# Unread transposes in TensorE's planned idle time, in the first ten head pairs of an attention and gated-FFN kernel

## The chip, the cores and the metric

The kernel runs on one core of a Trainium2 chip, as one program with one launch. The metric is the device time of an execution in microseconds; the figure shown is the median of several executions. The profile comes from one execution of its own, whose time and span are given below. In its views PE is TensorE (PEld its weight loads), DVE is VectorE, ACT is ScalarE, POOL is GpSimd, and SP issues most DMAs.

## What is computed

Attention over 8 batches of 8 heads, 576 positions and 64 channels a head, with rotary embedding of q and k, and after it a gated layer on the 512 joined channels, all in float32:

```python
q_rot, k_rot = (rotate(q), rotate(k))
scores = scale * np.matmul(q_rot, k_rot.transpose(0, 1, 3, 2))
scores = scores - np.max(scores, axis=-1, keepdims=True)
attn = np.exp(scores)
attn = attn / (np.sum(attn, axis=-1, keepdims=True) + 1e-09)
x = np.matmul(attn, v)                    # heads joined: (B, S, 512)
...
for k in range(K):                        # K = 5 taps, causal, one weight a channel
    gate_pre += conv_w[k][None, None, :] * xp[:, k:k + S, :]
gate = 1.0 / (1.0 + np.exp(-gate_pre))
val = x @ w_val
return gate * val @ w_out
```

## The kernel before

The work goes by **pairs** of heads: 32 pairs, four to a batch. A pair passes through these steps:

- **Rope.** k and q of the pair are loaded (L238), multiplied by tables and added (L255, L259, mostly on GpSimd), and split into a rounded high part (ScalarE, L262) and the rest (L266, GpSimd). The first pair's k is done on VectorE in part.
- **Scores.** `s_mm` (L283), five jobs a pair: four with rows of 128 for both heads (12 matmuls each), one with the last 64 rows of both heads (6 matmuls). A score tile takes two PSUM banks, and there are two of them. For each of nine tiles VectorE takes the negated maximum (L289), and ScalarE the exponential with its sum (L302).
- **Transposes.** `t_mm` calls `transpose` (L308): up to four 128x128 transposes of the exponentials into one PSUM bank of the pool `psT`, which a copy on ScalarE (L349) or VectorE (L351) takes to SBUF. This pool has four banks with one tag, shared with the products with V, the transpose of the sums and the gated layer.
- **Product with V.** `pv_mm` (L363), four jobs, 40 matmul instructions a pair. The sums are inverted (L374, L375), transposed (`r_mm`, L379), written to DRAM and read back spread over the partitions; VectorE multiplies them in (`x_norm`, L402).
- **Gate.** Split of x (L410, L414), five taps (L424 and L427, VectorE for four), tanh (L432).

After each fourth pair the gated layer of the batch follows, two stages of eight output tiles, each in three parts of four matmuls (`f_mm`, L450), between the attention jobs of the next pairs. The weights come as 64-bit words and are decoded on VectorE, GpSimd and ScalarE (`decode`, L486 to L500) during the first pairs.

**The order is a planner's.** Every step is a job with an engine, a duration written by hand, a due time (the table `DUE`), and the data that it reads and writes. `Plan.order` goes through them like a small scheduler: it starts the earliest job that can start, with lags between engines and the counts of buffers, and it keeps each job's planned `start` and `end` in nanoseconds. `Plan.run` then calls the jobs' functions in that order, and each engine executes its instructions in the order in which they were called:

```python
    def run(self):
        for i in self.order():
            self.jobs[i][3](*self.jobs[i][4])
```

The planned times themselves go no further: on the chip the engines wait for each other's semaphores alone. In the plan the first TensorE job, a score job, starts at 14.35 us. `ident` is a 128x128 identity that GpSimd builds at the start.

Of the kernel before, what the change touches and what calls it, by code (L numbers as in the profile page):

```python
# [10 lines left out]
F32 = mybir.dt.float32  # L11
# [43 lines left out]
class Plan:  # L55
# [10 lines left out]
    LAG = {"PE": 200, "V": 130, "A": 135, "G": 90, "SP": 100}  # L66
    WAIT = {"PE": 100, "V": 100, "A": 100, "G": 130, "SP": 40}
    SWITCH = 145

    def __init__(self):  # L70
        self.jobs = []
# [34 lines left out]
    def order(self, due=None):  # L106
# [34 lines left out]
        while len(done) < n:  # L141
# [11 lines left out]
            if m and m != mode:  # L153
                ns += self.SWITCH
                mode = m
# [17 lines left out]
        self.start, self.end = start, end  # L173
        return done

    def run(self):
        for i in self.order():
            self.jobs[i][3](*self.jobs[i][4])


# [1 line left out]
def attn_gated_ffn(ctx: ExitStack, tc: tile.TileContext, q2, k2, v2, tab, w_val, conv_w, w_out, out, collect=None):  # L182
# [14 lines left out]
    V, A, G, T, SP = nc.vector, nc.scalar, nc.gpsimd, nc.tensor, nc.sync  # L197
# [10 lines left out]
    psT = ctx.enter_context(tc.tile_pool(name="psT", bufs=B["ps_t"], space=PSUM))  # L208

    ident = const.tile([128, 128], F32, name="ident")  # L210
# [13 lines left out]
    state = {}  # L224
# [66 lines left out]
    def s_exp(p, i):  # L291
# [7 lines left out]
        else:  # L299
# [2 lines left out]
        A.activation(out=pd.rearrange("p (b x) -> p b x", b=2), in_=st[f"s{i}"], func=AF.Exp, bias=st[f"nm{i}"], scale=1.0,  # L302
                     accum_out=sums[p % 2][:, col:col + 1])

    def transpose(p, key, srcs):
        bank = psT.tile([128, 512], F32, name="ps_t", tag="ps_t")
        for j, (src, rows) in enumerate(srcs):
            T.transpose(out=bank[0:rows, j * 128:(j + 1) * 128], in_=src, identity=ident)  # L308
        state[p]["b" + key] = bank

    def t_mm(p, key):


        st = state[p]
        if key == "m":
            transpose(p, key, [(st["pm"][:, j * 128:(j + 1) * 128], 128) for j in range(4)])
        elif key == "hm":
            transpose(p, key, [(st["pm"][:, 448:S], 128)])
        elif key[0] == "h":
            g = int(key[1])  # L320
            transpose(p, key, [(st[f"p{2 * g + n}"].rearrange("p h s -> p (h s)")[:, 512:640], 128) for n in range(2)])
        else:
            c, h = int(key) // 2, int(key) % 2
            transpose(p, key, [(st[f"p{c}"][:, h, h * D + j * 128:h * D + (j + 1) * 128], 128) for j in range(4)])
# [218 lines left out]
    plan = Plan()  # L543
# [32 lines left out]
    for p in range(NP):  # L576
        t = 9 * p
        par = p % 2
        xt = toks(f"x{par}#@", R2)
        for n in ("k", "q"):  # L580
            cut = 320 if n == "k" else G0
            for a, b in [(0, W)] if p else [(0, cut), (cut, W)]:
                x = b - a
# [33 lines left out]
        for key, w in [(str(i), i) for i in range(8)] + [("m", 8), ("h0", 3), ("h1", 7), ("hm", 8)]:  # L617
# [7 lines left out]
            b = f"ps_t/{p}{key}"  # L625
# [7 lines left out]
        for g in R2 if last else (None,):  # L633
            k = "l" + str(g) if last else ""
# [5 lines left out]
        for g in R2:  # L640
            n = G1 if g else G0
# [14 lines left out]
        else:  # L656
            for g, (a, b) in enumerate(((0, G0), (G0, S))):
                x = b - a
# [11 lines left out]
        b = p // PPB  # L670
        last = b == NB - 1
        for stage in range(2):
            for j in range(8):
# [5 lines left out]
                key = f"f{stage}" + "l" * last + str(j)  # L679
# [9 lines left out]
                x = hi - lo  # L689
# [9 lines left out]
    if collect is not None:  # L699
        return plan  # L700
    with tc.manual_schedule():
        plan.run()


# [36 lines left out]
def _program(arrays, batches):  # L741
    import concourse.bacc as _bacc

    nc = _bacc.Bacc("TRN2", target_bir_lowering=False, num_devices=1)
    args = [
        nc.dram_tensor(f"in_{n}", a.shape, mybir.dt.from_np(a.dtype), kind="ExternalInput").ap()
        for n, a in arrays.items()
    ]
    args.append(nc.dram_tensor("out_t", (batches, DM, S), F32, kind="ExternalOutput").ap())
    with tile.TileContext(nc, schedule_with_timeline_sim=True) as tc:  # L750
        attn_gated_ffn(tc, *args)
    return nc
# [9 lines left out]
```

## Time and profile before

| what | value |
|---|---|
| median of 3 runs | 790.36 us (790.29, 790.36, 795.87) |
| profiled execution, its own time | 788.1 us |
| its span, first to last instruction | 786.3 us |
| instructions | 16022 |
| TensorE busy | 723.4 us (92% of the span), 5889 matmuls |
| VectorE, ScalarE, GpSimd busy | 542.2, 507.6, 538.1 us (69%, 65%, 68%) |
| mean granted TensorE clock | 0.967 |

How to read the views. A row of the slices gives the busy share of each of 40 equal slices in tenths; the clock row gives the granted TensorE clock in the same way. A row of the waits names the engine and tile that waited, what ended the wait, the total, the number of waits and the longest. A row of the stretches gives start and end in us, length, then for each engine its busy time and the number of instructions, the granted clock, the DMA share and GB/s. A row of the timeline gives start and duration in us, engine, line, operation, output and inputs, shapes and count of a group of like instructions, and in brackets the idle time before it and what ended it. The chain of waits follows the work that ended last back from the end; by line it gives shares of the stretch that is asked for.

### The profile page before, as it was taken

What the parts mean: (1) busy time and instruction counts of PE and PEld (TensorE: products, weight loads), DVE (VectorE), ACT (ScalarE), POOL (GpSimd) and SP (SyncE); (2) the same over time, 40 slices, a digit from 0 to 9 for tenths busy, and PEclk for the clock granted to TensorE, in tenths of its full rate; (3) what the DMA queues carried; (4) which work ended last, traced back from release to release, by engine and by line L of the source; (5) the groups of instructions that cost most, each with busy time, mean ns of one, the idle gap of its engine ahead of it and who ended that gap; (6) DMA issues with size and microseconds to landing.
All of it is one profiled execution on the core that took longest, in us unless ns stands there. A gap on an engine that the chain in (4) does not pass through costs nothing.

```text
span 786.3 us, 16022 instructions
## 1 busy us (share of the span) xinstructions
PE 723.4 (92%) x5889; PEld 582.9 (74%) x5889; DVE 542.2 (69%) x871; ACT 507.6 (65%) x1182; POOL 538.1 (68%) x395
## 2 busy tenths in 40 slices
PE   0687677999999999999999999999999999999998
PEld 0454454776789877787779878787778877887788
DVE  4769695788957767657767777656766876756750
ACT  1564544667677767766687667766687668766642
POOL 3788686787888776787757766777757866872021
PEclk9897677999999999999999999999999999999999
DMA  8454142243444233433443332333442343320101
GB/s 217 95 138 105 41 105 75 62 110 88 109 117 117 78 101 85 107 93 93 123 115 88 79 114 86 77 94 103 121 109 85 79 123 86 94 70 31 46 33 62
DMA packets 92881, 73.76 MB, mean 94 GB/s; under 512 B 60633, under 2 KB 71426, under 8 KB 92802
## 3 DMA queue, kind: packets, MB, share of 16 engines
q1 hardware_dynamic: 91250, 71.51, 34.1%
q10 hardware_dynamic: 1552, 1.21, 0.6%
q8 instruction: 47, 0.77, 0.4%
q14 instruction: 32, 0.26, 0.1%
HBM read 63.10 MB, written 9.59 MB: 92 GB/s over the span
## 4 chain that ended last, share of the span: by engine, by line
PE 76%; DVE 9%; ACT 6%; DMA 3%; issue 2%; SPq 2%; POOL 1%; DVEq 0%; ACTq 0%; POOLq 0%
PE ps_f L450 24%; PE ps_t L308 18%; PE ps_s L283 17%; PE ps_a L363 17%; ACT p L302 4%; DVE nm L289 3%; DMA rb<-rd 2%; DVE g L427 2%; SPq L238 1%; ACT pt L349 1%; POOL k L266 1%; DMA qin<-in_q 1%; DVE sums L374 1%; DMA v<-in_v 1%; DVE x L402 0%
## 5 line engine op out<-in xcount | busy, mean ns | idle before, releaser
L289 DVE TENSOR_REDUCE nm<-ps_s 128x1 f32<-128x576 f32 x288 | 208.1, 751 | 109.0 <-PE ps_s L283 107.7
L302 ACT ACTIVATE p<-ps_s,nm 128x576 f32<-128x576 f32 x288 | 212.1, 740 | 82.9 <-DVE nm L289 76.4
L308 PE MATMUL ps_t<-ident,p 128*128 128x128 f32 x1312 | 203.4, 289 | 35.2 <-ACT p L302 34.0
L308 PEld LDWEIGHTS ps_t<-ident,p 128*128 128x128 f32 x1312 | 152.7, 146 | 74.1 <-ACT p L302 50.4
L283 PE MATMUL ps_s<-k,q 64*128 64x288 f32 (+1 forms) x1728 | 178.9, 319 | 22.3 <-ACT k L262 17.6
L349 ACT COPY pt<-ps_t 128x512 f32<-128x512 f32 (+2 forms) x288 | 135.6, 477 | 67.7 <-PE ps_t L308 65.2
L283 PEld LDWEIGHTS ps_s<-k,q 64*128 64x128 f32 (+1 forms) x1728 | 139.4, 193 | 53.8 <-issue 25.0
L363 PE MATMUL ps_a<-pt,v 128*64 128x320 f32 (+1 forms) x1280 | 172.5, 418 | 0.0
L427 DVE SCALAR_TENSOR_TENSOR g<-x,cw,g 128x576 f32<-128x576 f32 (+2 forms) x132 | 137.7, 1044 | 1.3 <-ACT g L424 0.6
L363 PEld LDWEIGHTS ps_a<-pt,v 128*64 128x64 f32 x1280 | 88.2, 140 | 63.6 <-issue 13.0
L255 POOL TENSOR_TENSOR qin<-qin,tab_q 128x640 f32<-128x640 f32 (+2 forms) x66 | 106.8, 1632 | 37.0 <-DMA qin<-in_q 34.4
L450 PE MATMUL ps_f<-y,wout_hi 128*128 128x288 f32 (+2 forms) x512 | 107.9, 302 | 0.0
L255 POOL TENSOR_TENSOR kin<-kin,tab_k 128x640 f32<-128x640 f32 (+1 forms) x63 | 99.7, 1593 | 9.9 <-DMA kin<-in_k 9.9
L351 DVE COPY pt<-ps_t 128x512 f32<-128x512 f32 (+1 forms) x128 | 77.2, 615 | 20.8 <-PE ps_t L308 20.0
L414 POOL TENSOR_TENSOR xl<-x,xh 128x576 fp32r<-128x576 f32 (+2 forms) x33 | 46.1, 1397 | 62.8 <-ACT xh L410 62.7
L465 POOL TENSOR_TENSOR y<-y,y 128x288 fp32r<-128x288 f32 (+2 forms) x64 | 52.3, 820 | 51.5 <-ACT y L462 51.5
L450 PEld LDWEIGHTS ps_f<-y,wout_hi 128*128 128x128 f32 x512 | 81.5, 188 | 1.5 <-issue 1.5
L450 PE MATMUL ps_f<-xh,wval_hi 128*128 128x288 f32 (+2 forms) x256 | 78.3, 307 | 0.0
L450 PE MATMUL ps_f<-y,wout_lo 128*128 128x288 f32 (+2 forms) x256 | 77.2, 302 | 0.0
L450 PE MATMUL ps_f<-xh,wval_lo 128*128 128x288 f32 (+2 forms) x256 | 76.5, 300 | 0.0
L450 PE MATMUL ps_f<-xl,wval_hi 128*128 128x288 f32 (+2 forms) x256 | 75.5, 296 | 0.0
L266 POOL TENSOR_TENSOR q<-qin,q 128x640 fp32r<-128x640 f32 (+2 forms) x33 | 50.3, 1524 | 27.3 <-ACT q L262 27.3
(65 smaller groups left out, 782.8 us busy)
## 6 DMA issues: line engine op xcount, KB each, us to landing
kin<-in_k SPq DMA_DIRECT2D x62, 288.0 KB, 4.3
qin<-in_q SPq DMA_DIRECT2D x31, 512.0 KB, 5.0
out_t<-o SPq DMA_DIRECT2D x56, 144.0 KB, 2.2
rb<-rd SPq DMA_DIRECT2D x31, 144.0 KB
v<-in_v SPq DMA_DIRECT2D x32, 128.0 KB, 4.0
v<-in_v SPq DMA_DIRECT2D x64, 64.0 KB, 2.3
rb<-rd SPq DMA_DIRECT2D x31, 128.0 KB, 2.9
qin<-in_q SPq DMA_DIRECT2D x64, 32.0 KB, 3.8
```

The lines of the kernel that those rows point to most:

```text
L255: eng.tensor_tensor(out=t[:, i, a:b], in0=t[:, i, a:b], in1=tabs[n][:, i, a:b], op=ALU.mult)
L266: eng.tensor_tensor(out=t[:, 1], in0=ins[n][:, 0, a:b], in1=t[:, 0].bitcast(F32), op=ALU.subtract)
L283: T.matmul(out=tiles[h][:, half, 0:288], lhsT=st["q"][rows, x, c * 128:c * 128 + 128], rhs=st["k"][rows, y, k0:k0 + 288], start=(i == 0), ...
L289: V.tensor_reduce(out=st[f"nm{i}"], in_=st[f"s{i}"], axis=AX.XY, op=ALU.max, negate=True)
L302: A.activation(out=pd.rearrange("p (b x) -> p b x", b=2), in_=st[f"s{i}"], func=AF.Exp, bias=st[f"nm{i}"], scale=1.0, accum_out=sums[p % 2 ...
L308: T.transpose(out=bank[0:rows, j * 128:(j + 1) * 128], in_=src, identity=ident)
L349: A.copy(out=dst, in_=src)
L351: V.tensor_copy(out=dst, in_=src)
L363: T.matmul(out=acc[HEAD[h], 0:n], lhsT=st["v"][:, j, h, :], rhs=st[f"pt{g}"][:, at_:at_ + n], start=(j == 0), stop=(j == 4))
L427: V.scalar_tensor_tensor(out=g, in0=x_sb[:, a + k:b + k], scalar=w, in1=g, op0=ALU.mult, op1=ALU.add)
L450: T.matmul(out=acc[:, 0:n], lhsT=wt[w][:, kc, ds], rhs=mv, start=(kc == 0 and i == 0), stop=(kc == NCH - 1 and i == 2))
L465: G.tensor_tensor(out=ffn[b][1][:, dc, lo:hi], in0=ffn[b, "y", dc, lo], in1=ffn[b][0][:, dc, lo:hi].bitcast(F32), op=ALU.subtract)
```

## The change

`run` gets two more arguments, the function `t_mm` and a new function `fill`. It goes through the planned order as before. Ahead of each TensorE job it takes the planned idle time since the end of the TensorE job before it (since 3000 ns for the first), subtracts 300 ns and divides by 110 ns; the first job gets 25 more. If that number is over 2, the last TensorE job ended before 230000 ns in the plan, and one of the next four TensorE jobs (this one included) is a `t_mm`, it calls `fill` with that number and with the pair and key of that `t_mm`. `fill` takes the PSUM bank that this `t_mm` would take later, and issues that many 128x128 transposes of the identity into the first 128 columns of it. `transpose` then uses the bank that is there, and overwrites it. Nothing reads what `fill` wrote.

```diff
     SWITCH = 145
+    FILL = (3000, 230000, 300, 110, 25)
...
-    def run(self):
-        for i in self.order():
+    def run(self, turn, fill):
+
+
+        order = self.order()
+        pe = [i for i in order if self.jobs[i][1] == "PE"]
+        t, k = self.FILL[0], 0
+        for i in order:
+            if self.jobs[i][1] == "PE":
+                n = int((self.start[i] - t - self.FILL[2]) / self.FILL[3]) + (0 if k else self.FILL[4])
+                turns = [x for x in pe[k:k + 4] if self.jobs[x][3] == turn]
+                if n > 2 and t < self.FILL[1] and turns:
+                    fill(n, *self.jobs[turns[0]][4])
+                t = self.end[i]
+                k += 1
             self.jobs[i][3](*self.jobs[i][4])
...
+    def fill(n, p, key):
+        st = state.setdefault(p, {})
+        if "b" + key not in st:
+            st["b" + key] = psT.tile([128, 512], F32, name="ps_t", tag="ps_t")
+        for _ in range(n):
+            T.transpose(out=st["b" + key][:, 0:128], in_=ident, identity=ident)
+
     def transpose(p, key, srcs):
-        bank = psT.tile([128, 512], F32, name="ps_t", tag="ps_t")
+        bank = state[p].get("b" + key)
+        if bank is None:
+            bank = psT.tile([128, 512], F32, name="ps_t", tag="ps_t")
...
     with tc.manual_schedule():
-        plan.run()
+        plan.run(t_mm, fill)
```

## The prediction

> **What bounds the kernel now.** I read the slices first, then TensorE's waits before and after 141 us, the granted clock in stretches of 3.41 us, single groups of matmuls at both clocks, and the chain of waits in each stretch at half clock.
>
> ```profile
> PE   0687677999999999999999999999999999999998
> PEclk9897677999999999999999999999999999999999
> ```
>
> Each slice is 19.7 us. In the first seven TensorE is neither full nor at full clock; then it is full to the end. Before 141 us it waits for these:
>
> ```profile
> PE ps_t L308 <- ACT p L302: 28.2, 15, 3.5
> PE ps_s L283 <- ACT k L262: 17.6, 1, 17.6
> PE ps_s L283 <- ACT p L302: 2.8, 4, 1.1
> PE ps_s L283 <- POOL k L266: 1.2, 1, 1.2
> ```
>
> and after it for almost nothing (its largest wait from 141.20 on, then its busy time in the same stretch):
>
> ```profile
> PE ps_t L308 <- ACT p L302: 5.8, 9, 1.4
> ...
> 141.20:786.30 645.10, 633.65 (x5316) 518.92 (x5314) 444.59 (x708) 440.93 (x1033) 435.73 (x315) 1.00 0.33 90
> ```
>
> So from 141 us on 633.65 of 645.10 us is TensorE's own work at clock 1.00, in a fixed order. What is won before 141 us arrives at the end; nothing can be won after it.
>
> **Do transposes keep the clock up?** Columns: stretch, its length, TensorE busy (matmuls), clock, DMA. All matmuls first, then only those that write transpose banks.
>
> ```profile
> 25.14:28.56 3.42, 2.01 (x17) 1.00 0.83 239
> 31.97:35.38 3.41, 1.64 (x14) 1.00 0.01 2
> 38.80:42.21 3.41, 3.39 (x16) 0.50 0.17 16
> ...
> 134.37:137.78 3.41, 1.63 (x19) 1.00 0.71 174
> ...
> 141.20:144.61 3.41, 2.00 (x17) 1.00 0.00 0
> ```
>
> ```profile
> 38.80:42.21 3.41, 2.10 (x9) 0.50 0.17 16
> ...
> 134.37:137.78 3.41, 0.03 (x1) 1.00 0.71 174
> ...
> 141.20:144.61 3.41, 1.36 (x11) 1.00 0.00 0
> ```
>
> The stretches with 1.64 and 1.63 us busy (48%) were followed by half clock, those with 2.01 and 2.00 (59%) were not. The one from 134.37 holds 1.60 us of other matmuls and hardly a transpose, and the clock fell; the one from 141.20 holds 1.36 us of transposes and 0.64 us beyond them, and it stayed. If transposes did not count, it would be the other way round. Likewise 38.80 to 42.21, at half clock and mostly transposes, brought the clock back. I take it that transposes count, that the clock falls below a share between 48 and 59%, and that a full stretch restores it.
>
> [...]
>
> **What one transpose costs at each clock.**
>
> ```profile
> 17.63 2.27 PE L283 MATMUL ps_s<-k,q 64*128 64x288 f32 x12 [17.63 <-ACT k L262]
> ...
> 33.67 1.38 PE L308 MATMUL ps_t<-ident,p 128*128 128x128 f32 x8 [1.86 <-ACT p L302]
> ...
> 40.85 0.45 PE L379 MATMUL ps_r<-ident,sums 128*128 128x128 f32 x1
> ...
> 44.00 1.07 PE L283 MATMUL ps_s<-k,q 64*128 64x288 f32 x12
> ...
> 51.90 1.25 PE L308 MATMUL ps_t<-ident,p 128*128 128x128 f32 x10
> ...
> 61.89 2.40 PE L308 MATMUL ps_t<-ident,p 128*128 128x128 f32 x10 [1.71 <-ACT p L302]
> ...
> 157.44 0.30 PE L379 MATMUL ps_r<-ident,sums 128*128 128x128 f32 x1 [0.56 <-DVE sums L375]
> ```
>
> One alone lasts 0.30 us at full and 0.45 at half clock, so the step from one to the next is (1.25 - 0.30)/9 = 0.106 us at full and (2.40 - 0.45)/9 = 0.217 at half. The first score job's 2.27 us, part of it a wait for k, against the later 1.07 points to half clock there too, though the clock row shows 9: its records seem to begin later. Ten transposes lose 48% of their time when the clock is full; a score job that waits for nothing loses (1.81 - 1.07)/1.81 = 41% (the rows of 138.79 and 134.90 below). I use 42%, as score jobs hold most of the chain.
>
> **What the change adds.** No instruction goes. The plan's order is as before; `run` counts the plan's idle time before each TensorE job. Worked through with the file's costs, its rule gives 30 groups, 499 transposes: 125 ahead of the first score job, 374 in 29 groups up to pair 8, most of 13 to 20 ahead of transposes that wait for the exponentials. Such a group is hidden where the trace waits: 16 fills ahead of the job at 33.67 take 16 x 0.106 = 1.7 us of 1.86 idle. Four planned gaps, three before the product with V and one before the small transpose of pair 2's sums, have no transpose among the next four jobs and stay empty. Where other jobs stand between fill and real transposes, they are score jobs, which use other banks; the fill may wait for its bank's copy, with that score job queued behind it. I cost this at 0 to 0.5 us a place and take 0, since the real gaps there end later than the copies.
>
> **The gain, by the chain of waits.** The stretches at half clock, by lines of the chain (share of each stretch): 17.60 to 25.14, 35.38 to 42.21, 59.28 to 66.10; 76.34 to 83.17; 113.89 to 117.30, 120.72 to 130.96, 137.78 to 141.20.
>
> ```profile
> by line: PE ps_s L283 44.1%; PE ps_t L308 25.6%; ACT p L302 11.2%; DVE nm L289 10.2%; DVE k L266 8.9%; issue 2.1%
> by line: issue 36.6%; POOL q L266 22.5%; PE ps_s L283 16.5%; DVE nm L289 11.3%; ACT q L262 9.1%; ACT p L302 3.2%; ACTq L262 0.6%; POOLq L491 0.2%; DVEq L289 0.2%
> by line: ACT p L302 22.9%; DVE sums L374 22.4%; PE ps_a L363 20.2%; PE ps_s L283 15.4%; DVE nm L289 11.1%; PE ps_r L379 6.6%; DVE sums L375 3.3%; issue 3.0%
> by line: DVE nm L289 30.9%; PE ps_s L283 21.3%; DVE g L427 17.7%; PE ps_t L308 16.4%; ACT p L302 12.4%; DVE pt L351 8.8%; issue 2.1%; DVEq L289 0.3%
> ...
> by line: PE ps_s L283 69.4%; PE ps_t L308 37.5%
> by line: PE ps_t L308 34.2%; PE ps_a L363 21.6%; PE ps_s L283 17.4%; ACT p L302 16.4%; DVE nm L289 14.1%; issue 2.2%; PE ps_r L379 2.1%; ACTq L302 0.2%; DVEq L289 0.1%
> by line: PE ps_s L283 50.8%; PE ps_t L308 50.7%
> ```
>
> TensorE on the chain: 5.3 + 1.1 + 2.9 = 9.3 us up to 72; 2.6 in pair 2; 3.4 + 7.7 + 3.4 = 14.5 after 104. At 42% these are 3.9, 1.1 and 6.1, in all 11.1: the upper end. What is late next decides how much arrives:
>
> ```profile
> 72.07 0.93 PE L283 MATMUL ps_s<-k,q 64*128 64x288 f32 x10 [1.21 <-POOL k L266]
> ...
> 96.58 6.85 PE L363 MATMUL ps_a<-pt,v 128*64 128x256 f32 x40
> 103.36 1.06 PE L283 MATMUL ps_s<-k,q 64*128 64x288 f32 x12
> ...
> 134.90 1.07 PE L283 MATMUL ps_s<-k,q 64*128 64x288 f32 x12
> ...
> 138.79 1.81 PE L283 MATMUL ps_s<-k,q 64*128 64x288 f32 x12
> ```
>
> ```profile
> 43.00:60.00 17.00, 13.63 (x115) 9.64 (x111) 9.36 (x16) 10.01 (x23) 15.76 (x12) 0.98 0.62 160
> ...
> 104.00:120.72 16.72, 9.84 (x61) 7.69 (x57) 15.76 (x20) 9.29 (x20) 15.19 (x11) 0.80 0.30 70
> ...
> 120.72:130.96 10.24, 8.49 (x41) 6.34 (x43) 5.90 (x11) 6.01 (x14) 5.32 (x5) 0.50 0.19 60
> ```
>
> - **To 72 us, 0 to 3.9, taken 1.4.** Even with the slow clock TensorE waited 1.21 us for GpSimd's k there, and GpSimd was busy 15.76 of 17.00 us. It profits only as far as its own inputs, behind ScalarE's exponentials, come earlier.
> - **Pair 2, 0 to 1.1, taken 0.6**, for the same reason.
> - **From 104 on, 4.7 to 6.1, taken 5.4.** VectorE is busy 15.76 of 16.72 us until 120.72, so half of the 1.4 us of the stretch from 113.89 is given back to it; from 120.72 on no other engine stands near (VectorE 5.90, ScalarE 6.01, GpSimd 5.32 of 10.24 us).
>
> Sum 7.4. Costs against it:
>
> ```profile
> 1.01 0.29 POOL masks.py:199 TENSOR_SCALAR_AFFINE_SELECT ident<-ident 128x128 f32<-128x128 f32 x1
> ```
>
> The first block can start when the identity is there, at 1.3 us. With one slow stretch (3.4 us, 16 fills) it ends at 1.3 + 3.4 + 109 x 0.106 = 16.3; with two (31 fills) at 1.3 + 6.8 + 94 x 0.106 = 18.1, against the first score job's 17.63: 0 to 0.5 late, taken 0.3. The 25 fills ahead of the job at 103.36, which did not wait, take 2.7 us; a full clock in the product with V before it (40 matmuls in 6.85 us, of which 3.66 at half clock, up to 100.24) frees 42% of 3.66, 1.5: 0 to 1.2, taken 0.5. Twelve fills in three small groups of pairs 4, 5 and 8 stand where TensorE is full: 0 to 1.3, taken 0.6. Sum 1.4.
>
> Net 7.4 - 1.4 = 6.0: the profiled execution's 788.1 (span 786.3 and 1.8 around it) becomes 782.1. The median shown is 790.36, 2.3 higher. Part of that may be the phase of the slow stretches, which would vanish; I carry 0.9 over: **783.0 us**.
>
> **Rivals.**
> - **Given back (0.22): 787 to 790.** GpSimd and VectorE, both over 90% busy in the rows above, set the pace to 120 us; then only the last stretches' gain remains, and the fills' upper costs (0.5 + 1.2 + 1.3 = 3.0) eat most of it. For it: the wait for POOL k. Against: the chain after 120.72 is three quarters TensorE.
> - **The clock still falls (0.15): 785 to 788.** The change doesn't do what it says where gaps stay empty or VectorE is later than planned. One empty gap as long as the waits of 1.71 and 1.86 us above brings a stretch to the 48 to 59% at which it falls. Half of the stretches left gives half of 7.4, less 1.4: a gain of 2.3.
> - **All of it (0.12): 777 to 780.** GpSimd's and VectorE's inputs come earlier by as much, and the 11.1 arrive less small costs.
> - **Slower (0.06): 801 or more.** [...]
>
> **How the numbers follow.** The forecast has 0.45, with its own range 780 to 787. One per cent, about what a measurement of this kernel can tell from no change, is 7.9 us, so "faster" begins at 782.5: just under half of the forecast (0.22) and all of "all of it" (0.12), and a little from the tails, 0.36. "Slower" is the last rival and a rest for a bank that I mis-judged, 0.07; within 1% is 0.57. The range, 778 to 791, leaves out the slower rival and half of "all of it".
>
> **What would show it.** TensorE has 5889 + 499 = 6388 matmuls; the clock row is 9 in every slice after the first one or two; ten transposes of pair 1 take 1.25 us, not 2.40; the job that began at 134.90 begins some 6 us earlier, and the rest keeps that lead. If the clock is full and the lead at 72 us is nil, GpSimd sets the pace there. The forecast is wrong if the first score job starts well after 18 us, if half-clock stretches remain beside the empty gaps, or if TensorE's waits before 141 us turn into waits of score jobs for k.

## The result, and the profile after

Over 13 executions of each, the median went from 792.6 to 787.75 us. The ratio is **0.9936, with a 95% interval of 0.9912 to 0.9961**: 4.9 us less, under one per cent. Measured again later (below, with the gaps that stayed empty) the ratio was 0.9916, 0.9887 to 0.9944, with 5.1 us between the medians. The median of before, 790.36 when the prediction was made, is 792.6 with ten more executions; single ones lie between 789.86 and 796.33. The profiled execution after took 785.75 us, against 788.1.

The page after: span and instructions, busy time, the slices of TensorE, VectorE and the clock.

```profile
span 783.9 us, 17018 instructions
...
PE 760.3 (97%) x6388; PEld 623.9 (80%) x6388; DVE 553.6 (71%) x871; ACT 507.8 (65%) x1182; POOL 539.3 (69%) x395
...
PE   8899898899999999999999999999999999999998
...
DVE  4869797878866777656767767656766876756750
...
PEclk9999999999999999999999999999999999999999
```

There are 6388 matmuls, as counted. The clock is full in all 40 slices where before it fell in five of the first seven, and TensorE is nearly full from the first slice on. But **VectorE**, with the same 871 instructions, is 11.4 us busier than before (542.2), and the span is only 2.4 us shorter. Both hold for this pair of executions only. Each kernel was profiled a second time, on one chip (the runs stand at the end of the experiments); there VectorE is busy 547.3 us in both, and the span is 5.9 us shorter. I call the two profiles shown so far the first pair, and those the second. TensorE's waits before 141.20 us, after:

```profile
PE ps_t L330 <- ACT p L315: 6.7, 5, 1.6
PE ps_r L401 <- DVE sums L397: 2.0, 1, 2.0
PE ps_t L323 <- POOL ident masks.py:199: 1.4, 1, 1.4
PE ps_s L296 <- ACT p L315: 1.0, 1, 1.0
PE ps_s L296 <- ACT k L275: 0.9, 1, 0.9
PE ps_s L296 <- POOL k L279: 0.7, 1, 0.7
```

The 28.2 us of waits for the exponentials are 6.7 now. That is not a gain in itself: the fills stand there instead.

**Transposes count for the granted clock.** The first two stretches of the block (start, length, TensorE busy with its matmuls, clock; only these transposes run until 17.9 us), and the block:

```profile
1.36:4.77 3.41, 3.41 (x16) 1.00 0.70 167
4.77:8.18 3.41, 3.41 (x32) 1.00 1.10 259
```
```profile
1.36 15.62 PE L323 MATMUL ps_t<-ident 128*128 128x128 f32 x125 [1.36 <-POOL ident masks.py:199]
17.91 0.40 PE L296 MATMUL ps_s<-k,q 64*128 64x288 f32 x2 [0.94 <-ACT k L275]
18.56 0.93 PE L296 MATMUL ps_s<-k,q 64*128 64x288 f32 x10 [0.24 <-DVE k L279]
```

16 transposes fall in the first 3.41 us and 32 in the next. From the start of one to the start of the next it is 213 ns up to 4.8 us and 109 ns from 5.0 us on, close to the steps at half and at full clock before (217 and 106 ns): the clock doubled, with nothing but transposes on the engine. (The clock column shows 1.00 in both; its records begin at 5.0 us, so the first row's clock is read from the count.)

**Where the lead is won and lost.** The same jobs on TensorE, first before, then after: the end of pair 2's first score job, of pair 3's, of pair 4's; the first job of the gated layer; the transposes of pair 4's fifth tile.

```profile
72.07 0.93 PE L283 MATMUL ps_s<-k,q 64*128 64x288 f32 x10 [1.21 <-POOL k L266]
103.36 1.06 PE L283 MATMUL ps_s<-k,q 64*128 64x288 f32 x12
134.90 1.07 PE L283 MATMUL ps_s<-k,q 64*128 64x288 f32 x12
...
144.77 0.38 PE L450 MATMUL ps_f<-xh,wval_hi 128*128 128x288 f32 x1
...
149.90 0.60 PE L308 MATMUL ps_t<-ident,p 128*128 128x128 f32 x4
```
```profile
70.97 1.34 PE L296 MATMUL ps_s<-k,q 64*128 64x288 f32 x12
...
100.84 2.95 PE L323 MATMUL ps_t<-ident 128*128 128x128 f32 x25
103.72 1.07 PE L296 MATMUL ps_s<-k,q 64*128 64x288 f32 x12
...
131.85 0.93 PE L296 MATMUL ps_s<-k,q 64*128 64x288 f32 x10 [0.72 <-POOL k L279]
...
140.20 0.38 PE L472 MATMUL ps_f<-xh,wval_hi 128*128 128x288 f32 x1
...
146.61 0.66 PE L330 MATMUL ps_t<-ident,p 128*128 128x128 f32 x4 [1.14 <-ACT p L315]
```

And of the second pair, the end of pair 3's first score job and the last two of the list, first before, then after:

```profile
104.76 1.35 PE L283 MATMUL ps_s<-k,q 64*128 64x288 f32 x12
...
146.02 0.38 PE L450 MATMUL ps_f<-xh,wval_hi 128*128 128x288 f32 x1
...
151.14 0.60 PE L308 MATMUL ps_t<-ident,p 128*128 128x128 f32 x4
```
```profile
103.45 1.07 PE L296 MATMUL ps_s<-k,q 64*128 64x288 f32 x12
...
140.00 0.38 PE L472 MATMUL ps_f<-xh,wval_hi 128*128 128x288 f32 x1
...
146.40 0.65 PE L330 MATMUL ps_t<-ident,p 128*128 128x128 f32 x4 [1.12 <-ACT p L315]
```

| stage, up to | first pair: before, after | lead | won or lost | second pair: before, after | lead | won or lost |
|---|---|---|---|---|---|---|
| pair 2's first job | 73.00, 72.31 | +0.69 | +0.7 | 74.48, 72.88 | +1.60 | +1.6 |
| pair 3's first job | 104.42, 104.79 | -0.37 | -1.1 | 106.11, 104.52 | +1.59 | 0.0 |
| pair 4's first job | 135.97, 132.78 | +3.19 | +3.6 | 137.33, 132.57 | +4.76 | +3.2 |
| gated layer begins | 144.77, 140.20 | +4.57 | +1.4 | 146.02, 140.00 | +6.02 | +1.3 |
| pair 4's fifth tile | 149.90, 146.61 | +3.29 | -1.3 | 151.14, 146.40 | +4.74 | -1.3 |
| end of the span | 786.3, 783.9 | +2.4 | -0.9 | 789.5, 783.6 | +5.9 | +1.2 |

The last row of the table needs no cause in the change: from the fifth tile to the end, all but a little of it at full clock (1.00 from 160 us to the end in the first profile after, 1.00 from 141.20 us on in the first before), the two executions of before take 636.4 and 638.4 us, those of after 637.3 and 637.2. The losses that stand out are the 1.1 us of pair 2, in the first pair alone, and the 1.3 us behind the start of the gated layer, in both.

**What took the lead back.** VectorE before and after, around the first taps of pair 1 and then of pair 3, and GpSimd at the second of these times before, then at both after:

```profile
72.22 1.53 DVE L427 SCALAR_TENSOR_TENSOR g<-x,cw,g 128x576 f32<-128x576 f32 x2
...
146.07 0.28 DVE L486 TENSOR_SCALAR wst<-wst 128x256 int32<-128x256 int32 x1
146.27 0.81 DVE L427 SCALAR_TENSOR_TENSOR g<-x,cw,g 128x576 f32<-128x576 f32 x1
```
```profile
71.53 2.83 DVE L449 SCALAR_TENSOR_TENSOR g<-x,cw,g 128x576 f32<-128x576 f32 x2
...
141.50 1.02 DVE L508 TENSOR_SCALAR wst<-wst 128x256 int32<-128x256 int32 x1
142.44 2.18 DVE L449 SCALAR_TENSOR_TENSOR g<-x,cw,g 128x576 f32<-128x576 f32 x1
```
```profile
144.53 1.56 POOL L259 TENSOR_TENSOR kin<-kin 128x640 f32<-128x640 f32 x1
```
```profile
71.92 1.83 POOL L268 TENSOR_TENSOR qin<-qin,tab_q 128x640 f32<-128x640 f32 x1 [0.59 <-DMA qin<-in_q]
...
140.81 1.56 POOL L268 TENSOR_TENSOR kin<-kin,tab_k 128x640 f32<-128x640 f32 x1
142.45 1.56 POOL L272 TENSOR_TENSOR kin<-kin 128x640 f32<-128x640 f32 x1
```

A tap of 0.81 us lasted 2.18, until 0.6 us after GpSimd's addition from 142.45 had ended at 144.01; the decode step before it, 0.28 us, lasted 1.02, to just after GpSimd's multiplication ended at 142.37. Before, the same tap began at 146.27, after that addition had ended at 146.09. The maxima that the exponentials need stand behind these steps on VectorE, and TensorE's 1.14 us of wait at 146.61 is theirs. The second profile after has the same rows (the decode step and the tap, then the two taps of pair 1):

```profile
141.30 1.02 DVE L508 TENSOR_SCALAR wst<-wst 128x256 int32<-128x256 int32 x1
142.24 2.18 DVE L449 SCALAR_TENSOR_TENSOR g<-x,cw,g 128x576 f32<-128x576 f32 x1
```
```profile
72.12 1.67 DVE L449 SCALAR_TENSOR_TENSOR g<-x,cw,g 128x576 f32<-128x576 f32 x2
```

So the 1.3 us behind the start of the gated layer repeat, and with them the steps that make them: in both profiles the chain of waits runs from the tap over the maximum and the exponential to the transposes. The lead of TensorE has moved VectorE's steps against GpSimd's there. The 2.83 us of pair 1's two taps, 1.30 more than before, do not repeat. In the first pair the lead went from +0.69 at 72.31 to -0.60 at 76.01, where the transposes behind these taps began (75.41 before).

The taps that were stretched had started while GpSimd was in an operation, though not every such tap was. Of the 132 taps of VectorE in the first profile after, the 49 beside which no such operation ran took at most 0.82 us, as did the 22 that had begun before one; the 61 that started inside one (to 0.05 us) took 1.40 us in the median, 45 of them more than 0.9. How many start inside one differs from execution to execution: 59 and 64 before, 61 and 62 after, so over the program the change does not make them more.

From 20 to 160 us VectorE's busy time was 103.8 us before and 116.2 after, as the rows of that stretch show (TensorE, its loads, VectorE, ScalarE, GpSimd, clock; before, then after). In the second pair it was 104.7 and 112.2, with the same 547.3 us in the whole program: a part of the difference is work that comes earlier.

```profile
20.00:160.00 140.00, 103.76 (x695) 76.62 (x697) 103.82 (x162) 77.22 (x178) 109.54 (x81) 0.82 0.35 89
```
```profile
20.00:160.00 140.00, 126.21 (x1065) 102.32 (x1065) 116.15 (x165) 78.96 (x182) 114.55 (x83) 1.00 0.36 94
```

### The profile page after: what moved, and what is told of

Its sections match the earlier page's. It is cut to its first block, busy times and chain, and to the rows that moved or that the text cites. A ratio compares the mean times of both kernels' runs of the same rounds, so it can differ in the third digit from the quotient of the medians.

```text
span 783.9 us, 17018 instructions
## 1 busy us (share of the span) xinstructions
PE 760.3 (97%) x6388; PEld 623.9 (80%) x6388; DVE 553.6 (71%) x871; ACT 507.8 (65%) x1182; POOL 539.3 (69%) x395
## 4 chain that ended last, share of the span: by engine, by line
PE 76%; DVE 10%; ACT 5%; DMA 4%; issue 2%; POOL 1%; SPq 1%; DVEq 0%; ACTq 0%; POOLq 0%
PE ps_f L472 23%; PE ps_a L385 17%; PE ps_s L296 17%; PE ps_t L330 17%; DVE nm L302 3%; ACT p L315 3%; DVE g L449 2%; DMA rb<-rd 2%; PE ps_t L323 2%; ACT pt L371 1%; SPq L251 1%; POOL k L279 1%; DMA v<-in_v 1%; DVE wst L510 1%; DMA kin<-in_k 1%
## 5 line engine op out<-in xcount | busy, mean ns | idle before, releaser
L330 PE MATMUL ps_t<-ident,p 128*128 128x128 f32 x1312 | 194.4, 279 | 12.3 <-ACT p L315 10.2
L330 PEld LDWEIGHTS ps_t<-ident,p 128*128 128x128 f32 x1312 | 145.3, 141 | 49.7 <-ACT p L315 24.8
L296 PE MATMUL ps_s<-k,q 64*128 64x288 f32 (+1 forms) x1728 | 171.4, 309 | 2.9 <-ACT p L315 1.0
L385 PE MATMUL ps_a<-pt,v 128*64 128x320 f32 (+1 forms) x1280 | 168.7, 410 | 0.0
L296 PEld LDWEIGHTS ps_s<-k,q 64*128 64x128 f32 (+1 forms) x1728 | 133.8, 185 | 32.1 <-issue 23.0
L449 DVE SCALAR_TENSOR_TENSOR g<-x,cw,g 128x576 f32<-128x576 f32 (+2 forms) x132 | 142.7, 1081 | 1.3 <-ACT g L446 0.6
L385 PEld LDWEIGHTS ps_a<-pt,v 128*64 128x64 f32 x1280 | 86.5, 137 | 61.0 <-issue 8.9
```

The source lines that it names most:

```text
L296: T.matmul(out=tiles[h][:, half, 0:288], lhsT=st["q"][rows, x, c * 128:c * 128 + 128], rhs=st["k"][rows, y, k0:k0 + 288], start=(i == 0), ...
L385: T.matmul(out=acc[HEAD[h], 0:n], lhsT=st["v"][:, j, h, :], rhs=st[f"pt{g}"][:, at_:at_ + n], start=(j == 0), stop=(j == 4))
L449: V.scalar_tensor_tensor(out=g, in0=x_sb[:, a + k:b + k], scalar=w, in1=g, op0=ALU.mult, op1=ALU.add)
```

## The experiments

Ratios are to the kernel before on the same chip, with 95% intervals; the second profile of the kernel before is a single execution. The whole change was not run on the two chips of the first eight runs; it was on the chip of the last four.

**Which fills do it.** In `run`, the block ahead of the first score job alone, and the later gaps alone:

```diff
-                if n > 2 and t < self.FILL[1] and turns:
+                if k == 0 and n > 2 and t < self.FILL[1] and turns:      # block alone
+                if k and n > 2 and t < self.FILL[1] and turns:           # gaps alone
```

> Only the block of 125 ahead of the first score job is left; the 374 in the later gaps are not issued. Theory (the gain is the full clock in the later gaps, and a lead won before 46 us is lost there to the load of pair 2's q): 0 to 1.5 us faster than before, ratio 0.998 to 1.000, mean clock 0.96 to 0.98, with the falls to half clock of the kernel before from 31 us on. Rival (the warm start is what counts): 3 to 5 us, ratio 0.994 to 0.996.

> Only the 374 fills in the later gaps; no block at the start. Theory: 3 to 5 us faster than before, ratio 0.994 to 0.997; the first two or three groups run at 213 ns a fill until the clock is full and delay the first transposes by up to 1.7 us, of which nothing is left at 46 us. Mean clock 0.99 to 1.00. Rival (the warm start is what counts): 0 to 1 us, ratio 0.999 to 1.000.

Measured: the block alone **1.0013 (0.9991 to 1.0035)**, the gaps alone **0.9927 (0.9901 to 0.9953)**. The clock slices of the block alone:

```profile
PEclk9787776999999999999999999999999999999999
```

The block is worth nothing that can be measured: the clock falls after it as it does in the kernel before, or a little more (mean 0.952 to 0.965 in its executions, 0.959 to 0.970 in those of before). All of the gain that can be told from nothing is in the gaps, as the theory had it; by the ratio it is somewhat more than the 3 to 5 us of the theory, which the interval covers in part. The clock slices of the gaps alone are 9 throughout. Without the block, the first group of the gaps runs slowly and still does its work:

```profile
20.07 3.00 PE L323 MATMUL ps_t<-ident 128*128 128x128 f32 x16
22.91 0.60 PE L330 MATMUL ps_t<-ident,p 128*128 128x128 f32 x4
```

It is 3.00 us instead of 1.97. Contrary to what was expected, something is left of it in this trace: the first job of pair 1 begins at 44.41, in the whole change at 43.64, and pair 2's first job ends 0.45 us later. In the time it doesn't show. With the gaps alone one fall is left, after the 2 us before the transpose of pair 2's sums, which have no fill (timeline, then the stretches):

```profile
96.07 0.30 PE L401 MATMUL ps_r<-ident,sums 128*128 128x128 f32 x1 [2.03 <-DVE sums L397]
```
```profile
93.92:97.33 3.41, 1.38 (x13) 1.00 0.02 5
97.33:100.74 3.41, 3.41 (x20) 0.50 0.05 7
```

**How many fills, and until when.** No fill after 140 us of the plan; half of the fills in each gap; both:

```diff
-    FILL = (3000, 230000, 300, 110, 25)
+    FILL = (3000, 140000, 300, 110, 25)
-                    fill(n, *self.jobs[turns[0]][4])
+                    fill(n // 2 if k else n, *self.jobs[turns[0]][4])
```

> The limit of the plan's time goes from 230 to 140 us, so that the last five groups (32 fills, 3.5 us of TensorE) are gone. Theory of the prediction (12 of them stand where TensorE is full): 0.4 to 1.3 us faster than the changed kernel, ratio to before 0.992 to 0.9935. Rival (all of them hidden): the same as the changed kernel, 0.9936. If it is under 1 us, the runs will not tell it from nothing, and only the trace can.

> Half of the fills in each gap (the block at the start is whole). Theory (the clock falls below a busy share between 48 and 59% of 3.41 us): a gap of 2 us is filled by 0.9 us, the share is 70 to 80%, the clock stays at 0.99 or more and the gain is that of the changed kernel, ratio 0.992 to 0.996. Rival (the gate needs a nearly full stretch): mean clock 0.97 to 0.98, half of the gain, ratio 0.997 to 0.998.

> Both edits that cost no clock so far: half of the fills in each gap, and none after 140 us of the plan. If the fills that stand where TensorE is full cost something (3.5 us of its time in the whole change, half of it with half the fills), ratio 0.988 to 0.992, a little better than either alone; if not, 0.990 to 0.993 like either alone.

Measured: 0.9907 (0.9877 to 0.9937), 0.9908 (0.9877 to 0.9940), and 0.9910 (0.9881 to 0.9940) with both. None can be told from the whole change (0.9936 and 0.9916, on other chips), nor from another. Half of the fills is enough for the time, though not quite for the clock: 0.993 in the profile and 0.989 to 0.995 over the six executions, with three falls left in the profile, one of them after a stretch with 1.22 us busy of 3.41. The theory on the number held (a gain as large, a mean clock of about 0.99), but not its expected share of 70 to 80% in every gap. Its rival, in which the gate is what grants the clock, had expected 0.97 to 0.98. What the late fills cost stays below what these runs tell apart.

**Is VectorE with GpSimd the limit?** The decode of `w_out` was cut to 16 of 256 columns a step in both kernels, in `load_weight`. A constant takes the place of the weights, so these two kernels leave out the product with the real `w_out`:

```diff
+        y = x if n == "val" else 16
-        wsteps[n, i] = decode(st[:, 0:2 * x], st[:, 2 * x:3 * x].bitcast(F32), ...
+        wsteps[n, i] = decode(st[:, 0:2 * y], st[:, 2 * x:2 * x + y].bitcast(F32), ...
...
+        for w in (w_hi["out"], w_lo["out"]):
+            G.memset(w.bitcast(F32), 0.01)
```

> The kernel before, with the decode of w_out on VectorE and GpSimd cut from 256 to 16 columns a step (the weights are a constant instead, so this part of the result is left out); the plan and the order are unchanged. No theory needs a fixed time here: about 9 us of VectorE's and 14 us of GpSimd's work leave the first 170 us, and I expect 2 to 5 us less than before. It is the base for the next run.

> The same cut in the changed kernel (this part of the result is left out again). Theory (part of the lead that the full clock wins is lost because VectorE's steps are stretched while GpSimd is in an operation): with less of both the fills win 6.5 to 10 us over the lightened kernel before, against 4.9 between the two whole kernels. Rival (the lead is limited by the loads and by the fills themselves): again 4 to 6 us between the two.

Measured: 786.09 us (0.9933, 0.9907 to 0.9959) for the lightened kernel before, and 780.08 us (0.9847, 0.9819 to 0.9876) for the lightened changed kernel. The fills are worth **6.0 us** between the two medians and 6.8 by the ratios. The first is at the upper end of the rival's 4 to 6, the second inside the 6.5 to 10 of the theory, and neither can be told from the 4.9 between the whole kernels. The test doesn't show that this decode takes the lead, nor that it doesn't. What it shows is that both gains add up: 6.4 us between the medians by less decode, 12.4 by both. And the changed kernel's spread, 783.86 to 792.13 in 13 executions, shrinks to 778.33 to 780.88 in six; all six of these have a mean clock of 1.000, of the 13 only three.

**VectorE's copies to ScalarE.** In `t_copy` of the changed kernel:

```diff
+        eng = A if p < 5 else eng
```

> The changed kernel, with the copies of the transposes of the first five pairs all on ScalarE (four a pair of them were on VectorE, 0.6 us each). Theory (VectorE is late next): 0.5 to 2 us faster than the changed kernel, ratio 0.990 to 0.993. Rival (ScalarE's exponentials are late next, and the copies stand in front of them): 0 to 2 us slower than the changed kernel, ratio 0.994 to 0.997.

Measured: 0.9920 (0.9891 to 0.9950), with VectorE 15 us less busy than in the first profile after (538.3) and 9.0 less than in the second. It falls into the theory's band, but the changed kernel's own two measurements lie on both sides; nothing is shown.

**The gaps that stayed empty.** `fill` may also take the bank of the small transpose or of the product with V, with no fill after 140 us of the plan; and then all edits together:

```diff
-    FILL = (3000, 230000, 300, 110, 25)
+    FILL = (3000, 140000, 300, 110, 25)
...
-                turns = [x for x in pe[k:k + 4] if self.jobs[x][3] == turn]
+                turns = [x for x in pe[k:k + 4] if self.jobs[x][3] in turn and not (len(self.jobs[x][4]) == 3 and self.jobs[x][4][2])]
...
-        plan.run(t_mm, fill)
+        plan.run([t_mm, r_mm, pv_mm], fill)
```

> The changed kernel; the fill may also go into the bank of the transpose of the sums and of the product with V, so that the four gaps that stay empty in the change are filled too (none after 140 us of the plan). Theory (what is left of half clock comes from these gaps, above all from the 2 us before pair 2's sums): clock 0.999 to 1.000 in the profile, and 0.5 to 1.5 us less than the changed kernel on the same chip. Rival (the falls that are left are hidden behind VectorE): clock 1.000 too, and no difference in time.

> The edits together: the four gaps filled, half of the fills ahead of the transposes, none after 140 us of the plan, the first five pairs' copies on ScalarE. If VectorE is late next and the fills cost something, 2 to 4 us less than the changed kernel on the same chip, ratio to before 0.986 to 0.989; if neither, 0.990 to 0.993.

> The changed kernel once more, on the chip of the two kernels above: ratio 0.990 to 0.995; a second profile with a clock of 0.993 to 1.000, and VectorE's busy time 548 to 554 us.

Measured on one chip: all gaps filled 0.9945 (0.9921 to 0.9970), all edits 0.9944 (0.9918 to 0.9971), the change as it is 0.9916 (0.9887 to 0.9944), as expected. Filling the empty gaps brought nothing, as its rival had it; the clock was 0.998 in the profile, not the expected 0.999 or 1.000, with one fall left early. The combination, expected at 0.986 to 0.989, missed clearly; the 0.990 to 0.993 of the other case reaches into its interval. Its clock in the profile was 0.989; its slices:

```profile
PEclk9999898999999999999999999999999999999999
```

Over its nine executions the clock was 0.989 to 0.996, as with half of the fills alone (0.989 to 0.995), so the clock doesn't set it apart from that run. That these edits don't add up is what the run shows; why was not followed further. No version was found that is better than the change.

The second profile of the change has the same clock and nearly the same span as the first, with VectorE 6.3 us less busy, just under the 548 to 554 that were expected:

```profile
span 783.6 us, 17018 instructions
...
PE 760.4 (97%) x6388; PEld 623.9 (80%) x6388; DVE 547.3 (70%) x871; ACT 507.9 (65%) x1182; POOL 539.1 (69%) x395
```

**The kernel before once more.**

> The kernel before, once more, for a second profile of the same program. Theory (one execution differs from the next by how often VectorE's steps are stretched by GpSimd): the clock is 0.96 to 0.97 again, and VectorE's busy time moves with the span, 542 us at 786.3 us of span, 546 to 552 at 790 to 794. Rival (the phase of the clock's stretches makes the difference): VectorE's busy time stays within 2 us and the mean clock moves.

```profile
span 789.5 us, 16022 instructions
...
PE 723.3 (92%) x5889; PEld 581.5 (74%) x5889; DVE 547.3 (69%) x871; ACT 507.9 (64%) x1182; POOL 538.8 (68%) x395
```

The same program took 3.2 us longer with VectorE 5.1 us busier, at a higher mean clock (0.972 against 0.967). A part of that higher mean is the record alone: it begins at 30.2 us here and at 25.1 in the first profile, and what lies ahead of it counts as full, though the four transposes at 27.36 here still take 1.12 us, against 0.66 at 26.80. Between these two executions VectorE moved with the span, as expected; between the two profiles of the change it moved by 6.3 us and the span by 0.3.

Many executions speak for the rival. Of the 51 of the kernel before on the three chips of these experiments, the 14 with a mean clock of 0.957 to 0.961 have a median of 795.5 us, the 19 with 0.968 to 0.972 one of 790.8. Of the 19 of the change, the six with a clock of 1.000 have a median of 785.3 us, the 13 with 0.993 to 0.998 one of 787.8. Clock and time go together, from execution to execution; whether the clock leads, or a late VectorE makes the gaps in which it falls, these runs don't tell.

## Why the prediction was right, point by point

The time lies in the range, and the change is a gain of under one per cent. The range is wide, though: it holds the 790.36 of no change too. The point, 783.0 against 790.36, was a ratio of 0.9907; measured 0.9936 and 0.9916. The 787.75 us itself lies above the forecast's own 780 to 787, where two rivals are. A part of that is the base, which with ten more executions is 2.2 us higher; and of those rivals, the falling clock does not fit (0.993 and more in the executions after), and the early gain given back fits the first pair (a lead of -0.37 us at 104), not the second (+1.59). The slower rival's 801 did not come: the slowest of the 13 took 792.13. The 0.9 us carried over for the phase of the slow stretches was an estimate, and no run shows it by itself; what the runs show is that clock and time go together (795.5 us at 0.957 to 0.961, 790.8 at 0.968 to 0.972). By its steps, for the two pairs of profiles:

- **What is won before 141 us arrives at the end:** of 4.57 us at the start of the gated layer 2.4 in the first pair, of 6.02 all but 0.1 in the second. In both, 1.3 went in the next 5 us, where VectorE had no room (19.72 us busy of 20 from 140 to 160 in the first). The sum put nothing there: from 141 us on it took TensorE's own work as the only limit. What comes later is within what differs between executions of one program.
- **Transposes count for the granted clock:** shown, by the block (213 ns a transpose, then 109). In the clock's records of the first profile before, each stretch at one clock up to 141 us lasts 3.41 us or a multiple of it, up to 17.07. In all kept traces, from the first clock record to 260 us, the clock fell 41 times: 38 times after a stretch of 3.41 us at most 51% busy, three times after 54 to 58%. It stayed after three stretches of 45, 47 and 51%, the first of them, 1.54 of 3.41 us, in the changed kernel. So the bounds of 48 and 59% hold, but for the first two of these. The ten transposes of pair 1 that took 2.40 us before take 1.49 after; 1.25 was expected.
- **Fills are hidden where TensorE waits:** right. 16 fills ahead of the transposes at 33.67 take 1.91 us after, and these begin at 33.32.
- **To 72 us, taken 1.4 (less 0.3 for the block):** 0.7 and 1.6 came. GpSimd's k set the job there, as said. The first block, 0 to 0.5 late, ended at 16.98, before k was there.
- **Pair 2, taken 0.6 (less 0.5 for the 25 fills):** minus 1.1 and 0.0. In the first pair, the stretched taps of pair 1 (rows above) were not in the sum at all, and the 25 fills before 103.72 stood in the way: GpSimd's k was there at 102.75, so they cost about 1.0 where 0.5 was taken. In the second, k came at 103.13, and they cost about 0.3.
- **From 104 on, taken 5.4:** 4.9 and 4.4 came by the start of the gated layer. This term, read from the chain of waits at half clock, carries the gain. The job of 134.90 did not begin some 6 us earlier, as the signs had it: it ended 3.2 us earlier in the first pair and 4.8 in the second, and the lead of 4.6 and 6.0 stood a few us later.
- **Small groups where TensorE is full, taken 0.6:** the four ahead of a transpose at 229.84 moved it by their own 0.44.

So the mechanism and the main term were right. What the sum lacked in both pairs is VectorE at the start of the gated layer, minus 1.3 us: the next engine didn't only keep its pace, its steps lasted longer beside GpSimd's (1.02 us for 0.28, 2.18 for 0.81). The sum, 6.0, compares with 2.4 and 5.9 us for the pairs of executions and with 4.9 and 5.1 between the medians (6.7 by the second ratio). That the second pair meets it within 0.1 is luck: two executions of the same program differ by 3.2.

## What to carry to other kernels

Where TensorE idles in gaps of some 2 us, look at the granted clock in stretches of 3.41 us: here a stretch below about half busy was mostly followed by half clock (38 of 41 falls came after one at most 51% busy, and three such stretches had no fall behind them), and transposes that nobody reads kept it up (a mean of 0.993 to 1.000 in the 19 executions of the change, 0.957 to 0.972 in the 51 of before). They cost nothing where they ended before the real inputs came: 16 of them took 1.91 us, and the transposes behind them began at 33.32 us, against 33.67. Read the worth of it from the chain of waits in the slow stretches, not from the clock: here 26 us of TensorE's work at half clock on the chain were worth 5 to 7 us. And test which part of such a fill does it: the block at the start, a quarter of the fills, did nothing.

## What the runs showed that was not expected

- VectorE's steps that started while GpSimd was in an operation were often stretched: a tap of 0.81 us lasted 2.18, a decode step of 0.28 us 1.02, and 45 of 61 taps in the first profile after more than 0.9. When the steps meet differs between executions of one program; VectorE's total differs too (542.2 and 547.3 us before, 553.6 and 547.3 after), and a span of 783.9 or 783.6 us goes with either of the last two.
- A short wait was enough for the clock to fall: with the gaps alone, a single one of 2.03 us, in a stretch 1.38 of 3.41 us busy (40%), was followed by a stretch at 0.50.
- In the first profile after, TensorE began at half speed, although the clock's records show nothing until 5.0 us (25.1 us in the first before): 213 ns a transpose up to 4.8 us, against 109 from 5.0 us on.
